# The first chunk's x moved by 0/1 products, its squares on stacked blocks, w's sums for two batches at once, and all steps in another order

## The chip, the cores and the metric

One core of one Trainium2 chip runs the whole program. The metric is the device time of one execution in microseconds. Three executions of the kernel before took 642.71, 643.46 and 649.75 us, the median is 643.46 us. A fourth execution was taken with the hardware profiler, and all rows of the profile are of that one.

## The reference, cut to what matters

Two blocks follow each other. The first is a recurrence over 768 time steps with a 40 x 40 state for each of 4 batches and 8 heads; the second takes its output as 3072 tokens of 320 numbers (x), multiplies by `w_in` (320 x 2048), applies the exact gelu and multiplies by `w_out` (2048 x 320).

```python
for t in range(S):
    y[:, :, t] = np.einsum('bhd,bhde->bhe', rt, state)
    Sa = np.einsum('bhde,bhe->bhd', state, at)
    state_decay = state * wt[:, :, None, :] - np.einsum('bhd,bhe->bhde', Sa, bt)
    state = state_decay + np.einsum('bhd,bhe->bhde', vt, kt)
...
h = x @ w_in
g = 0.5 * h * (1.0 + erf(h * inv_sqrt2))
return g @ w_out
```

The weights `w_in` and `w_out` come in 64-bit floats; the kernel builds 32-bit floats from their words itself.

## The kernel before

The 768 steps are cut into 12 chunks of 64. Inside a chunk the recurrence becomes matrix products: running sums of log w give the decays, pairs of a, b, k, v, r are multiplied into 64 x 64 triangular matrices (one for each of 32 batch-and-head pairs), one of these has to be inverted, and the state goes from chunk to chunk. The names below are steps, functions that record instructions; the number behind a name is the chunk, and further numbers are halves or parts.

- **Loading.** `Lw`, `La`, `Lb`, `Lk`, `LV`, `Lr` load a chunk's inputs, `Lf` and `Lf5` load pieces of `w_in`, `Ls` pieces of `w_out`, all on SyncE's queue (SP). L443, L482, L533, L543 and L573 are their lines.
- **Decays.** `lg` takes the logarithm of w (L681), `wT` and `cu` sum it on TensorE against the triangle `cum_m`, `ew` (L724) and `ec` (L738) take exponentials, and `sb`, `sk`, `sa` scale b, k and a. `wT` makes, for every group of 40 columns, one 64 x 64 product for each of the two batches that lie in the two halves of the partitions.
- **Turning.** `ta`, `tb`, `tk`, `tr` turn tiles by transposes on TensorE (L747), `tv` by products with the unit matrix; `sn`, `kc`, `vc`, `rc` copy them out.
- **Triangles.** `nm`, `am`, `vm` are the 64 x 64 products, `nk`, `ak`, `vk` (L860) mask them.
- **The inverse.** For chunks 1 to 11 GpSimd does it by row operations (`iz`, `ic`, L957 and L959). For chunk 0 that would take too long, so it is done by repeated squares: `qt`, `qi` prepare the 32 x 32 blocks, `qm.0` to `qm.4` multiply on TensorE, and after each `qc`, `qz`, `qb` and `qa` copy, turn, mask and add on ScalarE and VectorE; `ql` and `qx` end it. `jm`, `jc`, `km`, `kt` join the 32 x 32 blocks to 64 x 64 ones.
- **State and output of the chunk.** `av`, `xm`, `sm`, `sc`, `pk`, `pb`, `oa` are products and sums; `om` (L1229) multiplies the output by the decays and writes it to `xt`, which is x turned. `xt` needs rows in another order than the one in which `om` writes: of each head pair 24 rows have to move to the other half of the partitions, and 16 rows of each pair are collected in a fifth tile. `ox` does this for every chunk by 11 small DMAs from `xt` to `xt` (L1241 and L1244).
- **The second block.** `mh` (L1305) multiplies x by `w_in`, eight parts for a chunk; `ge` (L1310) is the gelu; `pm` (chunk 0, L1426) or `m1` to `m7` (later chunks, seven products for what would be eight, L1344) multiply by `w_out`, with the sums `s1` to `s4` and `e1` to `e6` (L1295) around them; `so` and `sz` store.
- **Weights.** `ce`, `cs`, `cm`, `cv` (or `cl`, `cn`, `cx`, `cy`, `cg`) build 18 units of 32-bit weights. Units 0 to 4 are what `mh.0` needs first, 5 to 9 the rest of `w_in`, 10 to 17 `w_out`. The words of unit 9 lie in `xt` until they are built.

Tensor products run on TensorE in the order in which they are recorded, and so do the instructions of each other engine. That order is a list of some 1,450 steps, written out in `order()`; the program only adds the semaphores. On PSUM there are four double banks, given out in turn: a step that takes one waits until the step that held it two to four takes earlier has read it. `warm.4.n` and `warm_first` are products of nothing useful, put where TensorE was thought to be idle.

On TensorE the order between the first triangle and the first product of the second block is: nm.0 wT.1 cu.1 warm qm.0 ta.1 tb.1 nm.1 qm.1 cx.1 qm.2 tk.0 tv.0 qm.3 am.0 qm.4 tr.0 warm jm.0 vm.0 warm warm km.0 av.0 warm sm.0 tr.1 pk.0 pb.0 cu.2 tv.1 wT.2 vm.1 tb.2 tk.1 ta.2 nm.2 am.1 mh.0.2.

## Time and profile before

| | us |
|---|---|
| median of three executions | 643.46 |
| the profiled execution | 640.62 |
| its span (first to last instruction) | 638.7 |
| TensorE busy | 611.5 |
| VectorE busy | 456.4 |
| GpSimd busy | 378.3 |
| ScalarE busy | 331.6 |

Busy time counts an instruction from its start to its end. A product of 32-bit floats is recorded as two matrix instructions, so a row that says x64 is 32 products; a transpose is one. A group in the timeline is a row of like instructions merged; behind it, in brackets, stands the time for which the engine was idle before it, and what ended that time ("issue" where the profile shows nothing that was waited for). In the table by stretches each engine has its busy time and the number of its instructions; after the engines come the clock that TensorE was granted (1.00 is full speed), the busy share of the DMA engines and what they moved.

### The profile page before, as it was taken

The page shows a single profiled execution, that of the slowest core. Times are in us where ns is not written, and L with a number is a line of the kernel's source. Part 1 is how long each engine was busy: PE and PEld are TensorE (multiplying, and loading weights), DVE is VectorE, ACT ScalarE, POOL GpSimd, SP SyncE. Part 2 cuts the span into 40 slices and gives each one's busy share as a digit, 9 for nine tenths or more (in the row PEclk, how much of TensorE's full clock was granted, in tenths as well). Part 3 has the DMA queues.
Part 4 walks back from the last instruction along what each step waited for, and adds up shares of the span by engine and source line. Part 5 has one row for each costly group of instructions (what it writes and reads, how often), then busy time and mean ns, then how long its engine had stood idle before and what let it go on. Part 6 is the DMA issues. An engine that isn't in the chain of part 4 may idle for free.

```text
span 638.7 us, 31773 instructions
## 1 busy us (share of the span) xinstructions
PE 611.5 (96%) x14338; PEld 519.3 (81%) x14338; DVE 456.4 (71%) x557; ACT 331.6 (52%) x462; POOL 378.3 (59%) x782
## 2 busy tenths in 40 slices
PE   7689899989999999999999999999999999989997
PEld 4577688768988988988987987977988978978977
DVE  2789968996988879978885785976775874744213
ACT  4658867673444457446545554655643545243020
POOL 3368685828843876868968638848608838800000
PEclk9999899999999999999999999999999999999999
DMA  9997396946575752755683854376651620220100
GB/s 155 174 174 141 84 192 158 173 94 123 115 136 104 133 109 50 130 103 97 105 157 66 126 112 92 69 142 117 108 111 39 122 56 5 42 46 3 41 4 21
DMA packets 246914, 64.31 MB, mean 101 GB/s; under 512 B 228380, under 2 KB 243644, under 8 KB 246780
## 3 DMA queue, kind: packets, MB, share of 16 engines
q1 hardware_dynamic: 246340, 62.01, 52.0%
q8 instruction: 112, 1.84, 1.3%
q10 hardware_dynamic: 440, 0.29, 0.2%
q14 instruction: 22, 0.18, 0.1%
HBM read 54.39 MB, written 3.93 MB: 91 GB/s over the span
## 4 chain that ended last, share of the span: by engine, by line
PE 79%; SPq 6%; DVE 5%; DMA 4%; ACT 2%; issue 2%; DVEq 0%; ACTq 0%
PE bank L1305 32%; PE bank L1344 24%; PE bank L189 21%; SPq L443 3%; SPq L533 2%; PE bank L1426 1%; DMA xt<-xt 1%; SPq L1244 1%; DVE os L1295 1%; DMA xt<-in_moe_w_in_dram 1%; DMA VR<-in_v_dram 1%; DMA w_out_sb<-in_moe_w_in_dram 1%; ACT L738 1%; ACT conv L1259 1%; ACT part L738 0%
## 5 line engine op out<-in xcount | busy, mean ns | idle before, releaser
L1305 PE MATMUL bank<-xt,w_in_sb 64*64 64x256 f32 x3840 | 223.5, 380 | 2.2 <-DMA xt<-xt 2.2
L957 POOL TENSOR_TENSOR tmp<-W,Nb 128x126 f32<-128x126 f32 (+22 forms) x341 | 163.9, 481 | 77.3 <-DVE Nb L923 51.6
L1305 PEld LDWEIGHTS bank<-xt,w_in_sb 64*64 64x64 f32 x3840 | 153.4, 134 | 50.7 <-DMA xt<-xt 2.9
L959 POOL TENSOR_TENSOR W<-W,tmp 128x126 f32<-128x126 f32 (+22 forms) x341 | 165.1, 484 | 26.7
L1344 PE MATMUL bank<-w_out_sb,gt 128*128 128x160 f32 x704 | 100.8, 301 | 0.2 <-ACT gt L1310 0.2
L1344 PEld LDWEIGHTS bank<-w_out_sb,gt 128*128 128x128 f32 x704 | 96.6, 190 | 2.6 <-issue 0.9
L1310 ACT ACTIVATE gt<-bank 128x1024 f32<-128x1024 f32 x48 | 49.0, 1025 | 86.6 <-PE bank L1305 86.2
L1259 ACT COPY conv<-st 32x128 f32<-32x128 f32 (+2 forms) x55 | 28.0, 509 | 24.2 <-DVE st L1253 23.5
L1295 DVE TENSOR_TENSOR os<-os,bank 128x160 f32<-128x160 f32 x44 | 13.9, 316 | 34.1 <-PE bank L1344 24.2
L1171 DVE TENSOR_TENSOR SM<-bank,upper 128x832 f32<-128x832 f32 (+1 forms) x24 | 23.1, 988 | 15.2 <-PE bank L189 15.2
L1344 PE MATMUL bank<-extra,conv 128*128 128x160 f32 x208 | 30.4, 300 | 0.0
L1295 DVE TENSOR_TENSOR conv<-gt 128x1024 f32<-128x1024 f32 x11 | 14.3, 1303 | 22.0 <-ACT gt L1310 22.0
L717 DVE TENSOR_TENSOR_SCAN kT<-spare,kT 128x256 f32<-128x256 f32 x36 | 28.9, 859 | 0.8 <-ACT kT L710 0.8
L1344 PEld LDWEIGHTS bank<-extra,conv 128*128 128x128 f32 x208 | 28.8, 190 | 0.7 <-issue 0.5
L1223 DVE TENSOR_TENSOR st<-bank,st 128x832 f32<-128x832 f32 (+1 forms) x22 | 21.4, 987 | 8.5 <-PE bank L189 8.5
L1310 ACT ACT_TABLE_LOAD x19 | 24.4, 1283 | 4.7 <-PE bank L1305 4.4
L1344 PE MATMUL bank<-extra,gt 128*128 128x160 f32 x176 | 26.2, 302 | 0.0
L942 POOL MEMSET W<- 128x512 f32 x11 | 5.8, 525 | 33.7 <-DVE Tt L928 33.7
L785 POOL TENSOR_TENSOR bk_rows<-bk_rows,part 128x640 f32<-128x640 f32 x9 | 14.6, 1626 | 18.5 <-ACT part L738 16.5
L1344 PEld LDWEIGHTS bank<-extra,gt 128*128 128x128 f32 x176 | 24.4, 190 | 0.3
L738 ACT ACT_TABLE_LOAD x11 | 14.1, 1283 | 19.3 <-PE bank L189 13.8
L681 ACT ACT_TABLE_LOAD x11 | 14.1, 1283 | 17.8 <-DMA w_tile<-in_w_dram 17.1
(221 smaller groups left out, 1125.8 us busy)
## 6 DMA issues: line engine op xcount, KB each, us to landing
bk_rows<-in_b_dram SPq DMA_DIRECT2D x24, 160.0 KB
bk_rows<-in_k_dram SPq DMA_DIRECT2D x24, 160.0 KB
out_dram<-os SPq DMA_DIRECT2D x46, 80.0 KB
VR<-in_v_dram SPq DMA_DIRECT2D x22, 160.0 KB
w_tile<-in_w_dram SPq DMA_DIRECT2D x36, 80.0 KB
a_pairs<-in_a_dram SPq DMA_DIRECT2D x18, 144.0 KB
v_pairs<-in_w_dram SPq DMA_DIRECT2D x18, 144.0 KB
r_pairs<-in_r_dram SPq DMA_DIRECT2D x18, 144.0 KB
```

The source lines that it names most:

```text
L189: nc.tensor.matmul(o, lhsT, rhs, start=first, stop=True, skip_group_check=True)
L717: nc.vector.tensor_tensor_scan(logs[:, at:at + n], onward, logs[:, at:at + n], 0.0, ALU.mult, ALU.add)
L738: nc.scalar.activation(part_of(c), bank(f"cum{c}")[:, :, :DM], ACT.Exp, scale=-1.0)
L957: nc.gpsimd.tensor_tensor(t, W[:, BL // 2 - rows:, rest:rest + 1].to_broadcast([P, rows, rest]), Nb[:, rest:rest + 1, :rest].to_broadcast( ...
L959: nc.gpsimd.tensor_tensor(own, own, t, ALU.add)
L1171: nc.vector.tensor_tensor(SM[:, g, :, :, cols], pair_of(f"S{c}_", g).rearrange("p x i c -> p i x c")[:, :, :, cols], kept, ALU.mult)
L1223: nc.vector.tensor_tensor(to, pair_of(f"QY{c}_", g)[:, :, :, cols], to, ALU.add)
L1259: nc.scalar.copy(apart.rearrange("p e i g d -> p (e i g) d")[to_rows, :, to_col:to_col + n], st.rearrange("p e i g c -> p (e i g) c")[rows ...
L1295: nc.vector.tensor_tensor(to, one_, other, how)
L1305: nc.tensor.matmul(ph[half(x ^ y), x, s], w_in_sb[half(x), kt, at:at + HP], xt[half(x), kt], start=kt == 0, stop=kt == NK - 1, skip_group_ ...
L1310: nc.scalar.activation(gt[:, 4 * q:4 * q + 4].rearrange("p (x s) t -> p x s t", x=2), bank(f"ph{c}_{q}").rearrange("p x (s t) -> p x s t", ...
L1344: nc.tensor.matmul(po[:, n, :DM // 2], l_[:, f], r_[:, f], start=f == 0, stop=f == NF // 2 - 1)
```

## The change

Four things change.

1. For chunk 0 `om` writes to `first_x`, in the place of the turned r of chunk 0 (`rTs[0]`), and no longer to `xt`. `xp.0` and `xp.1` multiply `first_x` by matrices of zeros and ones (`moves`, set by GpSimd in the place of the turned r of chunk 1, `rTs[1]`), which puts each row where it belongs, and `xe.0` (ScalarE) and `xe.1` (VectorE) copy the two banks to `xt`. The 11 DMAs of `ox.0` are gone. Later chunks keep theirs.
2. The squares of chunk 0 work on the blocks as `nd.0` stacks them: ScalarE copies the lower diagonal blocks beside the upper ones, `qt` turns half as many columns, `qi` is one addition on 128 partitions (before: four on 32, two on GpSimd and two on VectorE), `qs` masks the turned blocks twice, and `qm.0` makes 32 products of 64 x 64 by 32 columns where there were 64 of 32 x 32.
3. `wT` multiplies all 128 partitions at once: 16 products by 128 columns where there were 32 by 64. Chunks 0 to 2 have this step.
4. The list of steps is another one throughout. On TensorE it now reads: nm.0 wT.1 ta.1 tb.1 warm qm.0 nm.1 warm warm tk.0 warm qm.1 am.0 cx.1 qm.2 warm tv.0 qm.3 warm tr.0 qm.4 vm.0 jm.0 av.0 km.0 tv.1 sm.0 pk.0 pb.0 tr.1 cu.2 xp.0 xp.1 wT.2 ta.2 tb.2 tk.1 vm.1 nm.2 mh.0.0 mh.0.1 am.1 mh.0.2 mh.0.3. Ahead of nm.0 stand warm_first warm cu.0 wT.0 warm tb.0 ta.0 warm cu.1; one more `warm` comes after tr.2. The loads of the first two chunks' w, b and a stand ahead of all pieces of `w_in`. Ahead of some steps other steps stand than before: cu.3 pm.0.3 av.2 ym.2 (before: av.2 cu.3 ym.2), cu.9 pk.8 pb.8 mh.7.1 av.9 (before: cu.9 am.9 pk.8), cu.11 mh.10.2 av.11 ym.11 (before: cu.11 av.11 ym.11).

Scratch tiles in DRAM and five steps that no list names are removed with it; they recorded nothing.

```diff
@@ places @@
+    first_x = rTs[0].rearrange("p g n t -> p (g n t)").rearrange("p (n t) -> p n t", n=NP)
+    flat_moves = rTs[1].rearrange("p g n t -> p (g n t)")
+    moves = flat_moves[:, :(2 + NP) * P].rearrange("p (m t) -> p m t", t=P)
+    diagonal = flat_moves[:, (2 + NP) * P:(2 + NP) * P + BL]
...
+    def moves_set():
+        nc.gpsimd.memset(moves, 0.0)
+        for m, to, at, n in ((0, 0, 0, D), (0, D, HP, REST), (0, HP, HP, D), (1, HP + D, 0, REST)):
+            nc.gpsimd.tensor_copy(moves[:, m, to:to + n], ident[:, at:at + n])
+        n = D - REST
+        for x in range(2):
+            for i in range(NP):
+                at = (1 - x) * HP + REST
+                nc.gpsimd.tensor_copy(moves[:, 2 + i, x * HP + i * n:x * HP + (i + 1) * n], ident[:, at:at + n])
...
     def wT(c):
-        pt = take(f"wT{c}").rearrange("p e (n t) -> p e n t", t=C)
+        pt = take(f"wT{c}").rearrange("p z (n t) -> p (z n) t", t=P)
         for n in range(G * NP):
             for x in range(2):
-                for e in range(2):
-                    at = (2 * n + x) * D
-                    mm(pt[half(x), e, n], logw[half(e), at:at + HP], cum_m[half(e), half(e)])
+                at = (2 * n + x) * D
+                mm(pt[half(x), n], logw[:, at:at + HP], cum_m)
...
+    stacked = flat(N_of(0))[:, :, :BL]
     def qt():
-        nc.vector.transpose(q_turned, flat(N_of(0)))
+        nc.vector.transpose(ZT, stacked)
-    def qi(z, q):
-        N = flat(N_of(0))
-        for rows, cols in quads[2 * z:2 * z + 2]:
-            engine_of_sum = nc.vector if q == "v" else nc.gpsimd
-            engine_of_sum.tensor_tensor(T_[rows], N[rows, :, cols],
-                                    ident[rows, rows].unsqueeze(1).to_broadcast([BL, NBL, BL]), ALU.add)
+    def qi(q):
+        eng = nc.vector if q == "v" else nc.gpsimd
+        eng.tensor_tensor(T_, stacked, diagonal.unsqueeze(1).to_broadcast([P, NBL, BL]), ALU.add)
...
     def qm(k):
-            if k == 0:
-                for rows, cols in quads:
-                    mm(pt[rows, n, :BL], q_turned[rows, n, cols], N[rows, n, cols])
-                continue
             for q in range(2):
-                if k == 4:
+                if k == 0:
+                    mm(pt[half(q), n, :BL], both_ZT[half(q), n], stacked[half(q), n])
+                elif k == 4:
...
+    def qs(z, q):
+        qb(-1, z, q)
...
     def om(c, g):
-        nc.vector.tensor_tensor(xt[:, :NP, g * P:(g + 1) * P].rearrange("p i (e t) -> p i e t", e=2),
+        to = xt if c else first_x
+        nc.vector.tensor_tensor(to[:, :NP, g * P:(g + 1) * P].rearrange("p i (e t) -> p i e t", e=2),
...
+    def xp(z):
+        pt = take(f"x{z}").rearrange("p a (n t) -> p a n t", t=TB)
+        mm(pt[:, 0], moves[:, 0], first_x[:, 2 * z:2 * z + 2])
+        if z:
+            for n in range(2):
+                mm(pt[:, 0, n], moves[:, 1], first_x[:, (2 * z + n + 1) % NP], False)
+            return
+        mm(pt[:, 0], moves[:, 1], first_x[:, 1:3], False)
+        for i in range(NP):
+            mm(pt[:, 1, 0], moves[:, 2 + i], first_x[:, i], i == 0)
+
+    def xe(z, q):
+        copy = nc.vector.tensor_copy if q == "v" else nc.scalar.copy
+        pt = bank(f"x{z}").rearrange("p a (n t) -> p a n t", t=TB)
+        copy(xt[:, 2 * z:2 * z + 2], pt[:, 0])
+        if z == 0:
+            copy(xt[:, NP], pt[:, 1, 0])
+        drop(f"x{z}")
```

## The prediction

> **What bounds the kernel now.** I read the page first, then the table by stretches, then what TensorE waited for.

> ```profile
> span 638.7 us, 31773 instructions
> PE 611.5 (96%) x14338; PEld 519.3 (81%) x14338; DVE 456.4 (71%) x557; ACT 331.6 (52%) x462; POOL 378.3 (59%) x782
> ...
> 0.00:77.50 77.50, 62.83 (x1594) 47.31 (x1594) 56.55 (x85) 52.75 (x71) 45.09 (x111) 0.99 0.83 146
> 77.50:160.00 82.50, 79.85 (x1948) 64.31 (x1952) 66.51 (x87) 54.37 (x77) 54.20 (x112) 0.97 0.72 147
> ```

> TensorE is busy for 611.5 of 638.7 us, so it sets the time: the span is its work plus its idle time, 27.2 us. Over half of that, 77.50 - 62.83 = 14.7 us, lies ahead of 77.5 us, where the first product of the second block begins. From there TensorE hardly stops, and a whole order that starts this dense part earlier ends earlier by as much, unless it leaves more work for later. So I price what TensorE has to do ahead of the dense part, what it waits for there, and what is left.

> ```profile
> 65.50 0.67 DVE L1229 TENSOR_TENSOR xt<-bank,wpT 128x512 f32<-128x512 f32 x1
> 68.02 3.76 SPq L1244 DMA_DIRECT2D xt<-xt  x4
> 74.39 3.14 SPq L1244 DMA_DIRECT2D xt<-xt  x4
> ...
> 73.78 1.16 PE L189 MATMUL bank<-aT,nT 40*64 40x64 f32 x64 [1.57 <-DVE aT L769]
> 74.74 1.26 PE L189 MATMUL bank<-aT,kT 40*64 40x64 f32 x64
> 77.52 11.32 PE L1305 MATMUL bank<-xt,w_in_sb 64*64 64x256 f32 x160 [1.53 <-DMA xt<-xt]
> ...
> 116.10 4.50 PE L1305 MATMUL bank<-xt,w_in_sb 64*64 64x256 f32 x80
> ```

> Between the last `om.0` (ends 66.17) and `mh.0` (77.52) lie 11.35 us and two rounds of DMA issues. But TensorE has other work there and waits for xt only 1.53 us. A second loss hangs on it: 160 matrix instructions of `mh.0` take 11.32 us, where 80 take 4.50 later, so 2 x 4.50 = 9.0; 2.3 us are lost. The clock tells why:

> ```profile
> 72.00:74.00 2.00, 0.43 (x15) 0.25 (x17) 2.00 (x3) 1.97 (x4) 0.45 (x2) 1.00 0.23 74
> 74.00:76.00 2.00, 2.00 (x128) 1.80 (x119) 1.97 (x5) 1.59 (x3) 0.33 (x1) 0.91 0.90 223
> 76.00:78.00 2.00, 0.48 (x4) 0.40 (x8) 2.00 (x3) 1.50 (x3) 1.92 (x2) 0.50 0.24 56
> 82.00:84.00 2.00, 2.00 (x40) 1.76 (x36) 1.81 (x4) 0.35 (x1) 1.76 (x4) 0.89 0.76 203
> ```

> TensorE was busy 0.43 of the 2 us from 72 and 0.48 of those from 76, and the granted clock fell to 0.50 until about 82.

> **What the parts cost.** The prices, on TensorE unless said otherwise:

> ```profile
> 7.50 1.34 PE L189 MATMUL bank<-w_tile,cum_m 128*128 128x320 f32 x4 [0.16 <-ACT w_tile L681]
> 10.49 1.16 PE L189 MATMUL bank<-cum_m,w_tile 64*64 64x64 f32 x64
> 16.92 1.16 PE L189 MATMUL bank<-aT,nT 40*64 40x64 f32 x64
> ...
> 33.88 0.65 DVE L1045 TENSOR_TENSOR turned<-turned,bank 128x512 f32<-128x512 f32 x1
> 38.27 1.97 PE L189 MATMUL bank<-ident,VR 128*64 128x128 f32 x32
> 34.62 0.57 ACT L1027 COPY turned<-bank 128x512 f32<-128x512 f32 x1
> 45.07 2.06 PE L189 MATMUL bank<-turned,st 64*64 64x32 f32 x64 [1.35 <-DVE turned L1045]
> 51.16 1.98 PE L189 MATMUL bank<-cum_m,ident 128*128 128x512 f32 x4
> 53.08 1.20 PE L189 MATMUL bank<-turned 32*32 32x32 f32 x64
> 55.05 1.66 PE L189 MATMUL bank<-VR,nT 64*64 64x104 f32 x64 [0.77 <-DVE VR L860]
> 69.37 1.97 PE L747 MATMUL bank<-ident,extra 128*128 128x128 f32 x16
> ```

> *x by products.* `xp` is three products of 512 columns (0.99 each, half of the 51.16 row) and six of 256, for which there is no row. Half of 0.99 is the lower end, 256/320 of the 7.50 row's 0.67 the upper: 0.50 to 0.54, and I take the lower, as the 512-column row is the same tile shape. Sum 3.0 + 3.0 = 6.0 us of TensorE that were not there. Against this stand the 1.53 us of waiting and the 2.3 us of slow clock. So the move alone does not pay on TensorE; it pays only if the order uses what it sets free. `xe` is one copy of 512 columns and one of 256 on ScalarE and one of 512 on VectorE, by the 34.62 and 33.88 rows under 1 us each, beside `wT.2` and `ta.2`. The 11 issues taken from SP's queue (from 66.2 to 77.5) let the `w_out` pieces start earlier. `moves_set` is 13 small GpSimd instructions, some 3 us ahead of `iz.1`; GpSimd was idle for 32 of the first 77.5 us, and what waits for it is `wx.1`, so I cost it at nothing; without that cover, 3 us.

> A wait is added: `rc.1` overwrites the place of `moves`, so it waits for `xp.1`, and `ew.2`, `ce.6` and `sn.2` are queued behind it on ScalarE, about 1.0 + 1.0 + 1.5 + 1.0 us, then `nm.2`. TensorE has wT.2, three turns and vm.1 there, 2.0 + 2.9 + 1.0 = 5.9 us, so it just fits.

> *w's sums.* `wT` gets the form of the 38.27 row, 16 products 128*64 by 128 columns: 1.97 for 1.16, +0.8 us three times. Fewer instructions, but more time.

> *Squares.*

> ```profile
> 19.52 3.03 POOL L1003 TENSOR_TENSOR turned<-N,ident 32x512 f32<-32x512 f32 x2 [13.22 <-DVE N L860]
> 20.33 0.34 PE L189 MATMUL bank<-cum_m,SM 64*64 64x64 f32 x8 [1.43 <-issue]
> 20.75 2.36 DVE L1003 TENSOR_TENSOR turned<-N,ident 32x512 f32<-32x512 f32 x2
> 24.60 0.32 PE L189 MATMUL bank<-N,st 32*32 32x32 f32 x14 [0.54 <-issue]
> 30.59 1.25 ACT L918 COPY spare<-spare 32x512 f32<-32x512 f32 x2 [0.44 <-DVE spare L860]
> 31.98 1.14 PE L189 MATMUL bank<-turned,st 64*64 64x64 f32 x31 [1.87 <-issue]
> ```

> `qi` falls from 2.36 on VectorE and 3.03 on GpSimd to one instruction of 512 columns, 0.65. In return `nd.0` puts 1.25 ahead of `qt`, `qs` some 0.7 behind it, and `qm.0` takes the 2.06 of the 45.07 row. On the chain to `qm.0` that is about even; VectorE is freed for `qz.0`.

> *The order.* Now the sum over TensorE's new list. Ahead of `nm.0`: cu.0 from 7.50, 1.34; wT.0 1.97; a warm 0.99; two flips 1.97; a warm 0.99; cu.1 1.34: `nm.0` at 16.1, 0.8 earlier than the row's 16.92. cu.1 needs chunk 1's w, now the fourth load, at 4 x 320 KB; by

> ```profile
> 0.00:10.00 10.00, 6.28 (x12) 2.61 (x12) 0.38 (x1) 4.01 (x4) 5.14 (x30) 1.00 0.83 128
> ```

> 1.28 MB have come by 10 us, so it is in time. From `nm.0` to `mh.0.0`: six triangles at 0.96 (73.78 to 74.74) 5.8; eight turns by flips at 0.98, 7.9; tv and wT, four at 1.97, 7.9; six warms 5.9; five squares 10.3; cx.1, as four 512-column instructions, 2.0; jm.0 and km.0 2.4; av, sm, pk, pb 6.6; cu.2 1.3; xp 6.0. Together 56.1 us. Before, the same stretch (16.92 to 77.52, 60.6 us) held 49 us of such work, by the same prices, and 11.6 us of waiting. After, I find these waits in the list:

> ```profile
> 47.96 0.71 DVE L1050 STREAM_TRANSPOSE st<-turned 128x512 f32<-128x512 f32 x1
> 50.23 1.18 ACT L1084 COPY turned<-bank 32x512 f32<-32x512 f32 x2 [0.54 <-ACT turned L1027]
> 53.00 2.48 ACT L1055 COPY Tt<-turned 32x512 f32<-32x512 f32 x4
> 59.57 1.94 DVE L1171 TENSOR_TENSOR SM<-bank,upper 128x832 f32<-128x832 f32 x2
> ```

> `jm.0` waits for `qa.4` and `ql` with only vm.0 between, 2 x 0.71 - 0.96 and a conversion ahead of them on VectorE, 1.0; `km.0` waits for qx, a copy of 0.6 and jc on ScalarE, 2.48 + 0.6 + 1.18, less ql, jm and av, 0.71 + 1.2 + 1.66: 0.7; `pb.0` waits for two `sc` less pk, 1.94 - 1.66: 0.4 with the handing over. That is 2.1 us. The other waits of before stand behind chains that now have a warm, `tk.0`, `nm.1` or `tr.0` in front of them. Three stalls of "issue" above, 3.84 us, came without any releaser in the stretch in which the DMA engines were nearly full; the new list has fewer instructions there but loads as much. Between none and all of them, I take one, 1.3 us. `mh.0.0` then starts at 16.1 + 56.1 + 2.1 + 1.3 = 75.6, 1.9 us earlier. But am.1 and one warm now come later, +0.96 + 0.99. The slow clock goes, -2.3, since the list has no gap of that length. The dense part shifts by -1.9 + 1.95 - 2.3 = **-2.3 us**.

> *Later waits.* Three waits of TensorE have one cause, a PSUM bank that `ec` still reads:

> ```profile
> 131.15 1.16 PE L189 MATMUL bank<-rT,turned 40*64 40x64 f32 x64 [1.07 <-ACT part L738]
> 441.00 1.66 PE L189 MATMUL bank<-VR,bk_rows 64*64 64x104 f32 x64 [1.27 <-ACT part L738]
> 568.90 1.16 PE L189 MATMUL bank<-rT,turned 40*64 40x64 f32 x64 [1.23 <-ACT part L738]
> ```

> Before ym.2, pk.8 and ym.11 at most one small product stood between `cu` and the step that takes its bank again. In the new list `pm.0.3` and `av.2`, 6 us, stand there at chunk 3, two state products and an `mh` at 9, an `mh` and `av` at 11: **-3.6 us**. What else idles past 77.5, 27.2 - 14.7 - 3.6 = 8.9 us, I leave as it is; the new list is as dense as the old, step by step.

> Sum: 638.7 - 2.3 - 3.6 = 632.8 us of span; with the 1.92 us around the span (640.62 - 638.7) 634.7. The profiled execution lies 0.44% below the median of 643.46, so in the median's terms 634.7 x 643.46 / 640.62 = **637.5 us**, 0.9% faster. One per cent is about what a measurement of this kernel can tell from no change; the forecast lies on that bound.

> **The rivals.**

> *The waits stay (slower).* TensorE's idle time ahead of `mh.0` is owed to the chain through VectorE, ScalarE and the loads, not to the x transfer, and the new order stands in it as long: then 16.1 + 56.1 + 11.6 = 83.8 for `mh.0.0`, +6.3, +1.95, and the slow clock stays: 646.9 of span, 651.7 in the median's terms if the later waits stay too, 648.1 if they go. For it: VectorE is busy 56.55 of 77.5 us and its list is no shorter; six warms are fixed work now. Against: the chain to `qz.0` loses the `qi` of 2.36 us. With the later gain it is slower than before from a start of `mh.0.0` at 77.5 + 3.6 - 1.95 = 79.2 us on.

> *All idle goes (faster).* No stall of "issue", and a quarter of the 8.9 us past 77.5 goes too: -1.3 - 2.2, 632.8 to 629.3, 634.0 in the median's terms. For it: fewer instructions ahead of 35 us. Against: the loads are as many.

> *The clock falls again.* The new list has ta.2, tb.2 and tk.1 in a row, as the old one had three such turns ahead of its fall, 69.37 to 72.2, then 1.57 us idle. If turns do not hold the clock, it falls again: +2.3, 635.1, 639.8 in the median's terms. [...] Against it, the three turns of the new list have vm.1 and nm.2 directly behind. [...]

> *The move is not what matters.* If xt had been late anyway, the 1.53 us would be the whole worth of it, and 6.0 us are paid: this is in the sum already.

> **How the numbers follow.** Forecast 0.55, split evenly by the 1% bound; all idle goes 0.14; the clock falls again 0.11; the waits stay 0.20. Faster by over 1%: 0.28 + 0.14 = 0.42; within 1%: 0.27 + 0.11 = 0.38; slower by over 1%: 0.20. Range: down past the faster rival by some 4 us for later waits that I left, 629; up to 650, between the slower rival's two figures.

> **What would show it.** Right: no xt-to-xt DMAs before 100 us, `xp` 6 us long, `wT` 2.0, `mh.0.0` at 74 to 77, clock 1.00 from 70 to 90, no wait for `part` behind chunk 3, 9 and 11, TensorE's busy time up by some 6 us (8.8 us of `xp`, `wT` and `qm.0`, less the 2.3) and its idle time down by 12. Wrong: `mh.0.0` past 79, a clock of 0.5 there, new waits of over 1 us past 160 us, above all where the output sums (`e`) free a bank.

## The result and the profile after

The changed kernel took 634.93 us (median of four executions, 634.23 to 637.49), the kernel before beside it 643.09 us (four, 640.58 to 649.75). The ratio is 0.988, 95% interval 0.984 to 0.992: 1.2% faster. The forecast was 637.5 us, a ratio of 0.991, and the range 629 to 650. All ratios here leave disturbed executions out, so one can lie some tenths of a per cent from the quotient of the medians.

The profiled execution is the slowest of the four, 637.49 us, where the profiled one of before, 640.62 us, was as fast as the fastest of its four (640.58). So the two spans differ by only 2.9 us, and a sum made from the two profiles misses some 5 us of the 8.2 between the medians.

The page of the changed kernel (span and engines), then its table by stretches:

```profile
span 635.8 us, 31493 instructions
PE 621.1 (98%) x14196; PEld 531.0 (84%) x14196; DVE 457.6 (72%) x558; ACT 337.5 (53%) x469; POOL 376.8 (59%) x797
```

```profile
0.00:77.50 77.50, 71.45 (x1258) 54.20 (x1258) 51.38 (x79) 51.35 (x70) 42.09 (x122) 0.93 0.91 154
77.50:160.00 82.50, 81.10 (x2159) 65.26 (x2161) 71.33 (x93) 64.27 (x88) 58.59 (x112) 1.00 0.70 142
```

TensorE is busy for 9.6 us more than before and idle for 14.7 us in place of 27.2. In the first 77.5 us its idle time fell from 14.7 to 6.1 us, but the mean clock there fell from 0.99 to 0.93. Its timeline, at the steps that the prediction priced:

```profile
15.88 1.16 PE L188 MATMUL bank<-aT,nT 40*64 40x64 f32 x64
...
22.90 2.08 PE L188 MATMUL bank<-N,st 64*64 64x32 f32 x62 [1.21 <-DVE st L1018]
...
51.30 1.48 PE L188 MATMUL bank<-st,N 32*32 32x32 f32 x64 [1.01 <-DVE st L1031]
...
64.11 1.65 PE L188 MATMUL bank<-SM,extra 64*64 64x104 f32 x61 [1.82 <-issue]
...
67.69 5.33 PE L188 MATMUL bank<-rT,rT 128*128 128x512 f32 x18
72.95 1.97 PE L188 MATMUL bank<-cum_m,w_tile 128*64 128x128 f32 x32
...
79.54 4.53 PE L1308 MATMUL bank<-xt,w_in_sb 64*64 64x256 f32 x80
```

`xp` takes 5.33 us. `mh.0.0` starts at 79.54, 2.0 us later than before, and TensorE comes to it without a wait and at full clock (1.00 from 78 to 80 us; 4.53 us for 80 instructions, before 11.32 for 160). From there to the end of the span it is 556.3 us, before it was 561.2. So in these two executions the gain lies behind the start of the second block, not ahead of it. Why the start is late, by the stretches of 2 us:

```profile
24.00:26.00 2.00, 2.00 (x78) 2.00 (x76) 1.27 (x3) 0.07 (x1) 2.00 (x6) 0.67 1.02 148
26.00:28.00 2.00, 2.00 (x32) 1.36 (x26) 1.65 (x3) 2.00 (x4) 0.34 (x2) 0.50 0.82 227
28.00:30.00 2.00, 2.00 (x3) 0.70 (x3) 1.90 (x6) 0.43 (x1) 0.00 (x0) 0.50 1.01 210
30.00:32.00 2.00, 2.00 (x10) 1.63 (x9) 1.56 (x4) 0.01 (x1) 0.00 (x0) 0.62 0.96 148
52.00:54.00 2.00, 2.00 (x63) 1.94 (x60) 1.93 (x5) 1.93 (x4) 1.86 (x7) 0.50 0.21 63
54.00:56.00 2.00, 2.00 (x70) 1.87 (x64) 1.44 (x3) 1.52 (x4) 1.83 (x3) 0.65 0.65 173
```

The clock fell twice to 0.50, behind the two short waits at 22.90 (1.21 us) and 51.30 (1.01 us). By an estimate from the granted clock of these rows, their 12 us held 6.9 us of work at full clock, so up to 5.1 us were lost. Over the four executions the mean clock of the span was 0.992, 0.992, 1.000 and 0.999: two of them had hardly any such fall. Their times, in the same order, are 637.49, 634.41, 635.46 and 634.23 us, so a fall did not always make the whole longer. The waits of TensorE that are left:

```profile
PE bank L188 <- issue: 4.1, 6, 1.8
...
PE bank L188 <- DVE st L1018: 1.2, 1, 1.2
PE bank L188 <- DVE st L1031: 1.0, 1, 1.0
...
PE bank L1347 <- ACT part L754: 0.3, 1, 0.3
```

The three waits for `part` (3.6 us before) are gone but for 0.3. The largest entry is "issue", time without a releaser, as it was before (5.1 us, 7 times).

### The profile page after: what moved, and what is told of

It is laid out like the page before. It is cut to its first block, busy times and chain, and to the rows that moved or that the text cites. A ratio compares the mean times of both kernels' runs of the same rounds, so it can differ in the third digit from the quotient of the medians.

```text
span 635.8 us, 31493 instructions
## 1 busy us (share of the span) xinstructions
PE 621.1 (98%) x14196; PEld 531.0 (84%) x14196; DVE 457.6 (72%) x558; ACT 337.5 (53%) x469; POOL 376.8 (59%) x797
## 3 DMA queue, kind: packets, MB, share of 16 engines
q8 instruction: 111, 1.82, 1.2%
## 4 chain that ended last, share of the span: by engine, by line
PE 90%; DVE 3%; SPq 3%; issue 2%; DMA 1%; ACT 1%; DVEq 0%; ACTq 0%
PE bank L1308 33%; PE bank L188 29%; PE bank L1347 25%; PE bank L1429 2%; PE bank L763 1%; SPq L469 1%; SPq L1226 1%; DVE os L1298 1%; DMA xt<-xt 1%; DVE st L1018 0%; DMA out_dram<-os 0%; SPq L1417 0%; SPq L1223 0%; DVE conv L649 0%; SPq L461 0%
## 5 line engine op out<-in xcount | busy, mean ns | idle before, releaser
L957 POOL TENSOR_TENSOR tmp<-W,Nb 128x126 f32<-128x126 f32 (+22 forms) x341 | 159.2, 467 | 86.0 <-DVE Nb L923 60.4
L959 POOL TENSOR_TENSOR W<-W,tmp 128x126 f32<-128x126 f32 (+22 forms) x341 | 168.5, 494 | 26.7
L1313 ACT ACTIVATE gt<-bank 128x1024 f32<-128x1024 f32 x48 | 49.1, 1024 | 86.9 <-PE bank L1308 86.6
L734 DVE TENSOR_TENSOR_SCAN kT<-spare,kT 128x256 f32<-128x256 f32 x36 | 26.0, 781 | 2.1 <-ACT kT L727 1.9
L1382 ACT COPY os<-bank 128x160 f32<-128x160 f32 x11 | 3.2, 290 | 44.7 <-DMA out_dram<-os 25.7
L1093 DVE COPY Tt<-bank 32x512 f32<-32x512 f32 x9 | 6.2, 689 | 22.3 <-ACT Tt L933 12.7
```

The source lines that it names most:

```text
L734: nc.vector.tensor_tensor_scan(logs[:, at:at + n], onward, logs[:, at:at + n], 0.0, ALU.mult, ALU.add)
L957: nc.gpsimd.tensor_tensor(t, W[:, BL // 2 - rows:, rest:rest + 1].to_broadcast([P, rows, rest]), Nb[:, rest:rest + 1, :rest].to_broadcast( ...
L959: nc.gpsimd.tensor_tensor(own, own, t, ALU.add)
L1313: nc.scalar.activation(gt[:, 4 * q:4 * q + 4].rearrange("p (x s) t -> p x s t", x=2), bank(f"ph{c}_{q}").rearrange("p x (s t) -> p x s t", ...
```

## The experiments

Two theories stood against each other. **Parts**: the three edited parts have costs of their own, by the rows of the prediction, and the order adds to them. **Places**: the parts are worth little, and what an experiment shows is where waits without a releaser fall. Times are medians of several executions beside runs of the kernel before on the same chip; the ratio to these, with its 95% interval, is what is compared.

| kernel | us | ratio to before |
|---|---|---|
| the changed kernel | 634.93 | 0.988 (0.984 to 0.992) |
| 1 old form of w's sums | 637.15 | 0.992 (0.988 to 0.995) |
| 2 x by DMAs, ahead of a's load | 644.15 | 1.002 (0.997 to 1.006) |
| 3 x by DMAs, behind a's load | 636.71 | 0.990 (0.987 to 0.994) |
| 4 x by DMAs, behind a's and k's loads | 638.18 | 0.990 (0.987 to 0.993) |
| 5 old squares | 642.27 | 1.001 (0.998 to 1.004) |
| 6 as 5, 128 instructions more, start late | 646.06 | 1.005 (1.002 to 1.007) |
| 7 as 5, 128 instructions more | 635.96 | 0.987 (0.983 to 0.992) |
| 8 changed, 128 instructions more, start late | 647.71 | 1.008 (1.005 to 1.010) |
| 9 before, 128 instructions more | 650.07 | 1.013 (1.010 to 1.016) |
| 10 without seven warms | 634.53 | 0.987 (0.982 to 0.992) |
| 11 the order with all three old parts | 640.43 | 0.992 (0.988 to 0.996) |
| 12 before, `cu` moved | 642.69 | 1.000 (0.998 to 1.002) |

### w's sums

```diff
-                mm(pt[half(x), n], logw[:, at:at + HP], cum_m)
+                for e in range(2):
+                    mm(pt[half(x), e, n], logw[half(e), at:at + HP], cum_m[half(e), half(e)])
```

> The changed kernel with wT and ew of before (32 products of 64 by 64 in place of 16 by 128 columns), everything else and the order unchanged. Theory 1, TensorE's list is the bound from the first triangle on, so each us of its work there counts: 3 x 0.8 = 2.4 us less, about 632.5 us where the changed kernel has 634.9. Theory 2, the first 80 us are set by chains through the other engines and the loads, and TensorE's work lies in their waits: within 1 us of 634.9.

The old form is 0.8 us shorter three times, yet the kernel was not faster: 0.4% slower by the ratios, though the two intervals overlap. In TensorE's timeline a long stall stands in the middle of `wT.1`, and even so the second block begins 2.5 us earlier than in the profile of the changed kernel (79.54):

```profile
19.95 0.34 PE L188 MATMUL bank<-cum_m,SM 64*64 64x64 f32 x7 [2.77 <-issue]
...
77.08 4.53 PE L1310 MATMUL bank<-xt,w_in_sb 64*64 64x256 f32 x80
```

What took the gain lies behind: from there to the end of the span it is 637.6 - 77.08 = 560.5 us, where the changed kernel has 556.3. Why that part became longer is not shown.

### x by products or by DMAs

```diff
-        to = xt if c else first_x
+        to = xt
 order():  moves_set, xp.0, xp.1, xe.0, xe.1 out;  2: ... ot.0.0 ox.0.1 ox.0.0 ... La.2
           3: ... La.2 ox.0.1 ox.0.0 ... Lk.2      4: ... La.2 ... Lk.2 ox.0.1 ox.0.0 Ls.0
           (cs.9 cm.9 cv.9 ahead of om.0, as unit 9's words lie in xt)
```

> The changed kernel with the first chunk's x moved by the 11 DMAs of before, issued where the products stood; om writes to xt again, and unit 9 is built ahead of it. Theory 1: 5.3 us of products go, but mh.0.0 has to wait for the DMAs, some 11 us from the last om, of which cu, wT, three turns and two triangles fill some 8; with 2.3 us for the clock if it falls there, the end moves by -2 to +1 us, 633 to 636. Theory 2, the transfer is what mh.0 waited for: mh.0.0 later by 3 us or more, 638 or more.

This run measured something else: SyncE's issues of `xt<-xt` waited for `om.0` (in the profile of before the first came at 66.24 us, 0.07 behind its end) and stood in front of the load of chunk 2's a. Kernel 2, SyncE's queue and TensorE:

```profile
63.23 1.72 SPq L1223 DMA_DIRECT2D xt<-xt  x2
...
68.31 2.41 SPq L1226 DMA_DIRECT2D xt<-xt  x4
...
71.54 1.36 SPq L461 DMA_DIRECT2D a_pairs<-in_a_dram  x2
```

```profile
77.31 1.94 PE L763 MATMUL bank<-ident,a_pairs 128*128 128x128 f32 x8 [11.89 <-DMA a_pairs<-in_a_dram]
```

> The changed kernel with its first chunk's x moved by the 11 DMAs again, this time queued on SyncE behind the load of chunk 2's a, so that TensorE's transposes of a do not wait behind them. om.0 ends at 67.5 us; before, 11.35 us lay between that end and the first product of the second block, so x is there at about 78. TensorE's list without xp ends at 79.5 - 5.3 = 74.2. Theory 1 (the move pays for itself only through the clock, and is worth about nothing): TensorE waits 3 to 4 us for the transfer, the second block starts at 77 to 78.5, the granted clock falls to 0.5 for some us, and the whole is -1 to +2 us of the changed kernel, 634 to 637. Theory 2 (the move carries the gain): 638 us or more, or a start after 80 us.

With a's load ahead of them, the same 11 DMAs cost 1.1% less (644.15 to 636.71 us). `mh.0.0` started at 74.25, earlier than expected, and did not wait for x at all. Then the next load in the queue, k's, was the late one. Kernel 3, TensorE, VectorE and SyncE's queue:

```profile
74.25 4.52 PE L1308 MATMUL bank<-xt,w_in_sb 64*64 64x256 f32 x80
81.65 1.99 PE L188 MATMUL bank<-aT,kT 40*64 40x64 f32 x64 [2.88 <-DVE N L876]
83.38 6.62 PE L1308 MATMUL bank<-xt,w_in_sb 64*64 64x256 f32 x80
```

```profile
79.55 0.82 DVE L801 TENSOR_TENSOR extra<-bk_rows,part 128x640 f32<-128x640 f32 x1 [6.11 <-DMA bk_rows<-in_k_dram]
```

```profile
70.58 3.52 SPq L1226 DMA_DIRECT2D xt<-xt  x4
74.63 2.20 SPq L461 DMA_DIRECT2D bk_rows<-in_k_dram  x2
```

The second `mh` group took 6.62 us for 4.52: the clock fell here as well, to 0.50 from 82 to 86 us. So I put the DMAs behind k's load too:

> The changed kernel with its first chunk's x moved by the 11 DMAs, queued on SyncE behind the loads of chunk 2's a and of its k. With them ahead of k's load, SyncE issued them from 65.5 to 74.1 us, k came late, VectorE waited 6.1 us for it and TensorE 2.9 us for VectorE, and the clock fell afterwards; x itself was not waited for (start of the second block 74.25). Theory 1 (the products are worth only what SyncE's queue costs those behind it): start of the second block at 74 to 76, no wait of TensorE for chunk 2's k, two parts of mh in 9.1 us, and the whole 1 to 4 us below the changed kernel: 631 to 634. Theory 2 (the products themselves carry a gain): 636 us or more, with TensorE waiting for x.

It came to 638.18 us, not to 631 to 634, and so into the range of theory 2. Whether TensorE waited for x, as that theory has it, is not known: the one profile is of an execution 7.5 us above the median, and nothing is read from it. Against either placing the products gain 0.2% by the middle values, with overlapping intervals: a worth of the move is not shown. In kernels 2 and 3 the DMAs cost what they held up in SyncE's queue, 11.89 and 2.88 us of TensorE's waiting, and that changed with where they stood.

### The squares, and a stall that moves

```diff
+            if k == 0:
+                for rows, cols in quads:
+                    mm(pt[rows, n, :BL], both_ZT[rows, n, cols], flat(N_of(0))[rows, n, cols])
+                continue
 order():  qs.0, qs.1, nd.0 out; qi in two halves (VectorE, GpSimd)
```

> The changed kernel with the first squares of before (blocks not stacked: four additions, a turn of 1024 columns, 64 products of 32 by 32), in the changed order. Theory 1: qm.0 is 0.4 us shorter, and its chain gets 2.4 us of VectorE, of which a warm hides 1: +0.5 to +1.5 us, 635.5 to 636.5. Theory 2, the chain through VectorE sets the start: +2 to +4 us, 637 to 639.

1.3% slower than the changed kernel, as slow as before, with this in TensorE's timeline, in the middle of `nm.1`, which is not one of the squares:

```profile
27.80 1.11 PE L188 MATMUL bank<-aT,nT 40*64 40x64 f32 x27 [4.36 <-issue]
```

The granted clock fell with it, to 0.54, 0.50, 0.50 and 0.75 in the four stretches of 2 us from 26 us on. The second of them:

```profile
28.00:30.00 2.00, 2.00 (x29) 1.36 (x25) 1.05 (x1) 0.00 (x0) 0.00 (x0) 0.50 1.01 213
```

The page has a row for the queue that brings instructions, of before first, then of the changed kernel:

```profile
q8 instruction: 112, 1.84, 1.3%
```

```profile
q8 instruction: 111, 1.82, 1.2%
```

A packet is 1.84 MB / 112 = 16 KB. The page of before counts 14338 matrix instructions and as many weight loads on TensorE: 2 x 14338 / 256 = 112.0; for the changed kernel, 2 x 14196 / 256 = 110.9. So, by an estimate from these rows, one packet brings 256 of TensorE's instructions. I counted them through each program: a product of 32-bit floats as four (two matrix instructions and two weight loads, as the trace records them), a transpose as two, and a wait as one, which is an estimate of mine. By this count the stalls of before and after stood 192 above a multiple of 256. If only the recorded matrix instructions and their weight loads are counted and the waits left out, every stall of over 0.15 us without a releaser, in every trace, falls short of such a place by 6 to 20 in the first 70 us (the three of before, at 20.33, 24.60 and 31.98 us, stand behind 440, 696 and 950, where the places are 448, 704 and 960), and by a number that grows to 116 by the end, which fits waits that add up. To test the count, it was shifted by 128, by cutting products that do nothing useful into smaller ones ahead of the first data:

```diff
 def warm_first():
-        for n in range(3):
-            mm(pt[:, n % 2], w_in_sb[:, 0, :P], w_in_sb[:, 0, :512])
+        for n in range(35):                                                    # 6 and 8
+            mm(pt[:, n % 2, :44], w_in_sb[:, 0, :P], w_in_sb[:, 0, :44])
...
+        for n in range(34):                                                    # 7
+            mm(pt[:BL, n % 2, :BL], w_in_sb[:BL, 0, :BL], w_in_sb[:BL, 0, :BL])
+        mm(pt[:, 0], w_in_sb[:, 0, :P], w_in_sb[:, 0, :512])
```

> The changed kernel with warm_first as 35 products of 44 columns where there are 3 of 512: the same work of nothing useful, ahead of the first data, but 128 more TensorE instructions ahead of everything (a product of 32-bit floats is four). Theory 1 (a stall without a releaser stands where TensorE's instruction count reaches 192 above a multiple of 256, as it does in all five traces so far, because the next block of instructions is not there): pb.0's stall of 1.82 us leaves its place near that step's third record. The new places are, by count, wT.0 record 18, wT.1 record 24, nm.1 record 36 of 64, am.0 record 22, tv.0 14, qm.4 35, km.0 35 and the third record of pk.0; if the first 35 us are where a block comes late, nm.1 gets a stall of 1 to 5 us. Time -1 to +4 us of the changed kernel. Theory 2 (the stall belongs to the step or its operands): it stays at the third record of pb.0, time unchanged within 1 us.

> The changed kernel with the old squares, whose trace had a stall of 4.36 us in nm.1 behind record 37, and the same 128 additional TensorE instructions ahead of everything. Theory 1 (blocks of 256 instructions): no stall at nm.1 behind record 37; by count the places are now wT.1 record 24, qm.0 record 101 of 128, then qm.1 22, qm.2 17, qm.3 46. A stall of 0 to 5 us at qm.0 or none; mh.0.0 moves accordingly, and with it the time: 638 to 643 us. Theory 2 (the old squares' chain makes the stall): 4 us at nm.1 as before, 642 us. If the time falls to 636 or below, the old squares cost nothing but the place of the block's end.

The small products were not the same work: TensorE's first group took 15.16 us, in the changed kernel 5.49, and `cu.0` began some 10 us late, so the times of 6 and 8 say little. The places say much. Kernel 6, the old squares, TensorE:

```profile
40.73 1.32 PE L188 MATMUL bank<-turned,st 64*64 64x64 f32 x38 [1.03 <-issue]
...
60.82 0.93 PE L188 MATMUL bank<-VR,nT 64*64 64x104 f32 x28 [0.38 <-issue]
...
66.09 1.56 PE L188 MATMUL bank<-SM,Tt 64*64 64x104 f32 x59 [0.73 <-issue]
...
69.82 1.65 PE L188 MATMUL bank<-SM,extra 64*64 64x104 f32 x61 [0.57 <-issue]
```

The count for these steps gives record 22 of `qm.1` (this one stands in the expectation), 35 of `av.0`, 2 of `sm.0`, 2 of `pb.0`. Seen: behind 23, 36, 3 and 3 (where the rest of 64 begins; a few records run into the next step's). The 4.36 us in `nm.1` are gone. In kernel 8 the stall at `pb.0` is gone too, and `km.0`, counted at 35, has one of 2.27 us behind record 36:

```profile
63.50 0.96 PE L188 MATMUL bank<-turned 32*32 32x32 f32 x28 [2.27 <-issue]
```

At the other four places that the expectation names for kernel 6, and the other seven for kernel 8, no stall shows. So one of the five named places had a stall in kernel 6, and one of the eight in kernel 8.

Then a form that delays the start less (`nm.0` at 17.32 us, in kernel 5 at 15.52):

> The changed kernel with the old squares and 128 more TensorE instructions ahead of everything, this time as 34 products of 32 x 32 by 32 columns and one of 512 columns in the place of the three of 512, which should end by 6.5 us and so delay nothing (the form with 35 products of 128 x 128 by 44 took 15.2 us and delayed the start by 10). The blocks of 256 instructions then end behind the squares at the same products as in the changed kernel. Theory 1 (the 7.3 us that the old squares cost are the place where a block ends in nm.1): no stall in nm.1, 635 to 638.5 us. Theory 2 (the old squares' chain costs it): 641 to 644 us, whatever the place.

635.96 us: the same squares, 6.3 us faster by the medians (1.4% by the ratios) for 128 more instructions of nothing, and no "issue" stall shown ahead of the second block, where kernel 5 has 4.97 us of them. What kernel 5 measured was in the main not the old squares but where its stalls fall. It was not the one stall alone: the shift moves all later places too, and the granted clock differs as well, 0.986 to 0.992 over the twelve executions of kernel 5 and 0.992 to 1.000 over the six of kernel 7. What share is the clock's stays open. New or old, the squares make no difference that these runs can tell (0.987 against 0.988).

The kernel before has places too:

```diff
 def warm(n, i):
+        if i == 20:
+            for m in range(33):
+                mm(pt[:BL, m % 2, :BL], ident[:BL, :BL], cum_m[:BL, :BL])
+        else:
             mm(pt[:, 0, :n * P], ident, cum_m.unsqueeze(1).to_broadcast([P, n, P]))
```

> The kernel before with its first warm as 33 products of 32 x 32 by 32 columns where there was one of 512 columns: 128 more TensorE instructions ahead of everything, in a stretch in which TensorE waits for w (0.2 to 0.6 us later at most). Theory 1 (the place where the blocks of 256 instructions end is worth some us to either kernel): the stalls of before at wT.1, qm.0, qm.1 and pb.0 (1.43, 0.54, 1.87, 0.31 us) leave these places; by count the places are wT.0 record 18, nm.0 56, qm.0 49, nm.1 32, qm.1 27, qm.2 50, qm.4 49, vm.0 39, av.0 35, pk.0 24; the time differs from the kernel before by over 2 us, to either side. If it falls by 5 us or more, all that the changed kernel gains could be had so. Theory 2 (in this order other waits end last, and a stall is made up): the stalls move, but the time stays within 0.3% of the kernel before.

It became 8.7 us slower (650.07 against 641.40 beside it), the most of all. Its second block begins at 77.84, only 0.3 later than in the profile of before. Nor does it begin earlier, though the stalls without a releaser ahead of it went from 3.84 us to 0.23: TensorE's idle time there fell by 3.1 us, and its busy time rose by 3.4, with a mean clock of 0.97 in place of 0.99. The loss lies past it. TensorE's timeline of kernel 9 from 100 to 450 us, the longest of its stalls without a releaser:

```profile
142.61 0.75 PE L189 MATMUL bank<-aT,nT 40*64 40x64 f32 x35 [1.87 <-issue]
...
252.96 0.21 PE L189 MATMUL bank<-T,Js 32*32 32x32 f32 x2 [1.58 <-issue]
...
332.78 0.27 PE L189 MATMUL bank<-rT,turned 40*64 40x64 f32 x2 [1.50 <-issue]
...
433.64 0.27 PE L189 MATMUL bank<-turned,N 32*32 32x32 f32 x9 [0.81 <-issue]
```

There are ten, 8.62 us in all. Before has two in the same stretch:

```profile
237.98 0.85 PE L189 MATMUL bank<-aT,nT 40*64 40x64 f32 x42 [0.21 <-issue]
...
420.30 0.42 PE L189 MATMUL bank<-st,aT 40*64 40x104 f32 x9 [0.36 <-issue]
```

The difference is 8.05 us; from the start of the second block to the end, kernel 9's profile is 10.9 us longer (572.1 against 561.2). Behind the two longest stalls the clock fell as well, to 0.54 and 0.50, and behind the first of them 39 instructions of `mh` took 3.58 us, where 40 take 2.34 at 187.10. Behind the one at 332.78 the work was hardly slower: the next group, 16 instructions of 160 columns, took 2.44 us, where such a group took 2.34 ahead of it. The clock behind the two longest:

```profile
144.00:146.00 2.00, 2.00 (x28) 1.99 (x23) 1.90 (x2) 1.19 (x2) 0.00 (x0) 0.54 0.93 195
...
254.00:256.00 2.00, 2.00 (x24) 1.17 (x20) 1.81 (x2) 1.30 (x2) 1.69 (x5) 0.50 0.03 8
```

Some 100 ends of 256 lie behind the start of the second block (2 x 12744 / 256). By an estimate from the records of the two traces about 39 of them lie in parts of `mh` in before and about 21 in kernel 9; the shift moved the others into shorter products, triangles and 32 x 32 blocks among them, where the longest stalls stand. In both kernels most of the ends show no stall: the whole profile of before has 7 without a releaser, that of kernel 9 has 12.

### The warms

```diff
 order():  without warm.4.1 warm.4.15 warm.4.18 warm.4.24 warm.4.4 warm.4.20 and warm.4.0
```

> The changed kernel without the six warms between the first triangle and mh.0.0 and without the one after tr.2 (they compute nothing that is used). Theory 1, TensorE's list is the bound there: up to 6.9 us less, about 629, less what opens as waits, so 629 to 632. Theory 2, chains are the bound: within 1 us of 634.9. Theory 3, the warms hold the clock: it falls to 0.5 for longer in the first 60 us and the time rises, 636 to 640.

The second block began at 75.03 us, 4.5 earlier, but the rest of the profiled span was 2.6 us longer (558.9), and the median was the same (634.53). TensorE's busy time fell by 7.1 us and its idle time rose by 5.2: waits opened in the chain of the squares, 2.00 us at `qm.0`, 0.82, 1.07. The clock fell behind them (mean 0.78 from 22 to 26 us, 0.50 from 26 to 30) as it did with the warms. They neither cost nor save anything that can be told.

### The order

> The changed order with the old form of all three parts (w's sums by batch, old squares, x by DMAs behind chunk 2's loads of a and k). Measured one by one against the changed kernel the old parts cost +2.2 us (sums), +7.3 (squares), +1.8 (x, behind a only). Theory 1 (each part has its own cost): 635 + 2.2 + 7.3 + 0 to 1.8 = 644 to 646, so the order alone gains nothing. Theory 2 (most of the 7.3 us is where TensorE's blocks of 256 instructions end, and these lie elsewhere here): 636 to 641, so the order carries most of the gain.

The changed order with all three old parts (the three diffs above together) took 640.43 us, 0.8% faster than before. Old parts that cost 0.4, 1.3 and 0.2% one by one cost 0.4% together, so their costs are not their own. In its profile the second block starts 2.4 us later than in that of the changed kernel, but the rest is the shortest of all, 637.8 - 81.89 = 555.9 us:

```profile
25.31 0.63 PE L188 MATMUL bank<-N,st 32*32 32x32 f32 x26 [1.86 <-issue]
...
81.89 5.18 PE L1315 MATMUL bank<-xt,w_in_sb 64*64 64x256 f32 x80
```

The stall again lies where it was counted, behind 102 of `qm.0`'s 128 records (101 by the count). Two longer ones, 2.04 and 2.77 us, stand in `wT.1` and `pb.0`.

```diff
 order() of before:  cu.3 ahead of pm.0.3, ec.3 ahead of av.2; cu.9 ahead of mh.7.6; cu.11 ec.11 ahead of mh.10.2
```

> The kernel before with cu.3, cu.9 and cu.11 (and ec.3, ec.11) put earlier in the list, as the changed kernel has them. Theory 1 (each of the three waits for a PSUM bank behind ec was lost time): the waits before ym.2, pk.8 and ym.11 go, -3.6 us, ratio to the kernel before 0.994 to 0.995. Theory 2 (something else is late there next): the waits go but others of the same length open within some 10 us behind them, ratio 0.998 to 1.002.

No gain: 1.000 (0.998 to 1.002), where 0.994 was forecast. The waits for `part` did fall from 3.6 to 0.5 us, and from `mh.0` to the end the profiled execution was 2.7 us shorter. But it began 4.4 us later, though no instruction ahead of it had changed, with a clock that fell where it had been 1.00 in the profile of before:

```profile
30.00:32.00 2.00, 1.96 (x32) 1.44 (x33) 0.70 (x2) 0.00 (x0) 0.00 (x0) 0.81 1.41 112
32.00:34.00 2.00, 2.00 (x4) 0.67 (x2) 2.00 (x5) 1.19 (x2) 0.42 (x2) 0.50 1.08 198
...
46.00:48.00 2.00, 2.00 (x19) 1.94 (x18) 1.22 (x2) 0.00 (x0) 1.69 (x5) 0.50 0.44 106
```

So the start of the second block differs by over 4 us between executions of the same instructions, and a single profile can't measure a gain of 2 or 3. Twelve executions can, and they show none. Why the three waits were worth nothing is not settled.

## Why the prediction was right, and where not

The forecast (0.9% faster) lies inside the interval, and two of its sums came out: TensorE's idle time fell by 12.5 us (12 forecast), and from `mh.0` to the end 557.3 us were forecast (561.2 + 1.95 - 2.3 - 3.6) where 556.3 were measured. That the whole came so near is in part luck. Between the two profiles the span fell by 2.9 us, where 5.9 were forecast: TensorE's busy time rose by 9.6 us instead of some 6, with the clock falling. And the larger term of the sum, -3.6 for the later waits, was worth nothing where it was tried alone (kernel 12). Point by point:

- **x by products, "the move alone does not pay on TensorE".** Right: kernels 3 and 4 lie within 0.2% of the changed one. `xp` was forecast at 6.0 us and took 5.33: the three products of 512 at 0.99 leave 2.36 for the six of 256, 0.39 each, under my lower end of 0.50. What I had not seen is what the DMAs cost others: 11.9 us of waiting for a in kernel 2, 2.9 in kernel 3.
- **`moves_set` at nothing, and the wait of `rc.1` that "just fits".** Both held: no wait stands before `nm.2`.
- **w's sums, "more time", 0.8 us three times.** The duration was right (1.97), the sign for the kernel was not shown: the old form was no faster. Its 192 additional instructions move all later ends of 256, so kernel 1 does not tell what the form alone is worth.
- **Squares about even.** Right, though kernel 5 alone would have said the opposite; kernel 7, whose ends of 256 behind the squares lie at the same products as the changed kernel's, shows them even.
- **The order, `mh.0.0` at 75.6.** Wrong for the profiled execution, 79.54, past the 79 that I had named as the mark of a wrong step. `nm.0` came at 15.88 (16.1 forecast), the waits were 1.2 + 1.0 us where I had 2.1, the stall 1.8 where I had 1.3. What was missed is the clock: it fell at two places that I had not thought of, up to 5.1 us. Two of the four executions had hardly any such fall; when their second block began is not recorded. A profile is one draw, and I had taken it for the kernel.
- **"A whole order that starts this dense part earlier ends earlier by as much."** Not borne out. Kernel 10 starts at 75.03 and ends as the changed one; kernel 3 starts at 74.25 and is no faster; kernel 11 starts at 81.89 and has the shortest rest. The changed kernel itself was to be slower than before from a start at 79.2 on, and was faster with 79.54.
- **Slow clock at 72 to 82, -2.3.** Right: 1.00 there, 9.06 us for 160 instructions.
- **Later waits, -3.6.** The waits went. That their going is the gain is contradicted by kernel 12. The rest of the span did become 5 us shorter with the new order (556.3 and 555.9 against 561.2), but by which of its moves stays open.
- **"Between none and all" of the "issue" stalls, one.** Near by chance: 2.05 us came ahead of the second block. I had taken them for the loads' doing alone and not asked what decides their place. Their place is worth more than any part of this change: 6.3 us (kernel 5 to 7) and 8.7 us (before to 9) for 128 instructions.
- **The rivals.** "The waits stay" fell, by the idle time. "The clock falls again" came true, but elsewhere and not in each execution. Its condition, that turns do not hold the clock, no run shows. In the changed kernel the fall at 24 us follows two turns and a wait of 1.21 us; kernel 3 has the same two turns, no wait behind them, and keeps its clock:

```profile
20.00:22.00 2.00, 2.00 (x30) 1.24 (x29) 1.97 (x4) 1.97 (x4) 0.89 (x1) 1.00 1.06 213
22.00:24.00 2.00, 2.00 (x102) 2.00 (x102) 1.71 (x2) 1.35 (x3) 1.84 (x4) 1.00 1.16 212
24.00:26.00 2.00, 2.00 (x29) 1.04 (x19) 1.97 (x5) 1.75 (x3) 0.35 (x2) 1.00 1.08 159
```

  Before had two such turns with waits of 1.16 and 1.87 us behind them, and kept it as well:

```profile
30.00:32.00 2.00, 0.13 (x5) 0.02 (x2) 0.55 (x1) 1.38 (x3) 0.00 (x0) 1.00 1.13 175
32.00:34.00 2.00, 2.00 (x33) 1.47 (x34) 0.77 (x2) 0.01 (x1) 0.00 (x0) 1.00 1.00 216
```

  Nor is the second wait enough by itself: kernel 6 has it too, 1.00 us ahead of `jm.0`, and its clock stayed at 1.00 throughout.

How much of the 1.2% is the order and how much the places of the ends of 256 in the two programs stays open: one shift by 128 moved either kind of kernel by as much as the change did (1.4 and 1.3% by the ratios, the change 1.2%), only one shift was tried on before, and on the changed kernel itself none that left its start in place. The granted clock is mixed into it: of the 27 executions of before beside kernel 3 the fastest, 639.16 us, had a mean clock of 0.994, the slowest, 645.95 us, 0.986.

## What to carry to other kernels

Where one engine is nearly always busy, undoing a part of a change also shifts every instruction behind it; before a part is credited with the difference, shift the unchanged program by as many instructions and see whether it moves as much. What a transfer taken off a queue was worth here depended on what stood behind it in that queue (TensorE waited 11.89 us with a's load behind the DMAs, 2.88 with k's), so its old form has to be tried at more than one place. One profile shows where time goes, but not gains below the spread between executions.
